# The first four units of chunk 0 in plain float32, block means from full value tiles, and a new order, in a fused attention and feed-forward kernel

## The chip, the cores and the metric

The kernel runs on one core of a Trainium2 chip. The metric is device time in microseconds (us), the median of several runs. The engines, as the profile names them: PE (TensorE; PEld is its loading of weights), DVE (VectorE), ACT (ScalarE), POOL (GpSimd) and SP (SyncE, which here issues nearly all transfers). Each works through its own list of instructions in order and waits on the others by semaphores.

## The reference, cut to what matters

Inputs: q, k, v of shape (4 batches, 8 heads, 768 tokens, 64), float32; w_in (512 x 2048) and w_out (2048 x 512), which arrive as float64.

```
k_sum = k in blocks of 32 tokens, max over the block        # 24 block keys per head
v_sum = v in blocks of 32 tokens, mean over the block       # 24 block values
scores = q.k / 8 where |i - j| < 16, else -1e9 ;  q.k_sum / 8 + log(32)
a = exp(scores - max) ; a = a / (sum(a) + 1e-9)
x = a @ concat(v, v_sum)                                    # 3072 tokens x 512 (8 heads x 64)
h = x @ w_in ;  g = h / (1 + exp(-h)) ;  out = g @ w_out
```

## The kernel before, in words

**Tiling.** A *stage* s is 128 tokens of all heads: batch b = s // 6, tile t = s % 6, 24 stages. A *chunk* c is two stages, 256 tokens; there are 12. A *unit* (c, f) is one chunk through one pair of 128-wide blocks of the hidden layer, f = 0 to 7. The units of chunks 0 to 3 come first, in the order chunk 0 f 0 to 3, chunk 1 f 0 to 3, chunk 1 f 4 to 7, chunk 0 f 4 to 7, then chunks 2 and 3; from chunk 4 on the chunks go in pairs with seven products in place of eight (another function). Stages 0 to 3 are called plain (`s < NPL`): their attention is in float32.

**Attention of a plain stage.** PE multiplies q by the local keys and by the block maxima `km` (scores, L722); the maxima come from DVE (L473) over K tiles that hold a whole batch of two heads. DVE adds the mask and takes the row maximum (L747), ACT takes the exponential (L751), PE transposes, ACT or DVE copies, and PE multiplies by the value tile (L792), whose last 24 rows are the block means. The sums of the exponentials are turned into factors, spread over the partitions by PE (`over`), copied to `xr`, and multiplied by the value product (L846): that is x.

**Block means.** `job_mean` (L630) adds six tiles of values times a small matrix of 1/32 into one bank on PE (L649) and takes each tile's largest absolute value on DVE (L652). For tiles 0 to 3 it reads the value tiles that attention uses too (`main_v`, L616), which hold 94 rows in two overlapping halves, so there are two matmuls to a tile, with the matrices `blocks0`, `blocks1` and `blocks2`; tiles 4 and 5 are loaded apart, 128 rows, one matmul each with `blocks`. The result is copied to `vms` (L653) and SP stores it into the value tiles (`side_v`, L625/626). The largest value gives the scale of x (`v_scale`).

**Weights.** A weight comes as float64, 1 MB. ACT rescales its top words (L922), one of three engines its low words (L923), DVE joins them to float32 (L924, `plain_w`). For the first layer the largest value follows (L940, PE L944, DVE L948), and from it a power of two `ur`; then the weight is split in two float16 halves (`split_w`, L956 and L957).

**A unit.** The first layer adds three float16 products (high x high, high x low, low x high; L1006, 24 matmuls of 256 columns to a unit). So x has two halves as well: `xh` (L848) and the remainder `xl` (L849), both in the scale taken from the means' values. ACT takes tanh(h/2) with its scale (L1020), DVE forms (1 + tanh) * h (L1021). In chunks 0 and 1, f below 4, ACT multiplies by `ur` (L1023) and the second layer is plain float32 with `plain_w` (L1015, 128x512); elsewhere g is split as x is and the second layer is three float16 products.

**What sets the order.** `Plan` collects operations, each with a cost for every engine that may run it. The string ORDER, three characters an operation, names the next operation and its engine; since it covers all 2679 operations it is replayed as it stands (`replay`). The costs then decide only how the lists of different engines are laid beside one another as they are issued, and how many filler matmuls (into bank 0, without use of their result) go between PE's operations until the first chunk has begun. SP's queue is in order as well. Buffers for loading (`staging`) are taken from weight buffers whose weights come later: `staging(-1)` and `staging(0)` name which.

SP's list before, from the start: q, K tiles, the value tiles between them, q, three more value tiles, the first weights (f 0 first layer and second layer, f 1 both); then the stores of `vms` into the value tiles, and the rest of the weights.

Of the kernel before, what the change touches and what calls it, by code (L numbers as in the profile page):

```python
# [21 lines left out]
P = 128  # L22
# [43 lines left out]
class Plan:  # L66
# [14 lines left out]
    DMA0 = 800.0  # L81
# [46 lines left out]
    def sweep(self, prio, on, back):  # L128
# [7 lines left out]
        free = {} if back else {"dma": self.DMA0}  # L136
# [122 lines left out]
def local_attn_ffn(ctx: ExitStack, tc: tile.TileContext, q0, qkT, qF, qkD, kF, v0, v, vR, w, out):  # L259
# [57 lines left out]
    blocks1 = const.tile([P, 11 * 4], F32, name="blocks1")  # L317
    blocks2 = const.tile([P, 11 * 4], F32, name="blocks2")
    nc.vector.memset(blocks1, 0.0)
    nc.vector.memset(blocks1[:, 19:24], 1.0 / BLK)  # L320
    edge = blocks1[:, 19:24]
    nc.gpsimd.affine_select(out=edge, in_=edge, pattern=[[-BLK, 5]], compare_op=ALU.is_ge, fill=0.0, base=BLK - HALO, channel_multiplier=1)
    nc.gpsimd.affine_select(out=edge, in_=edge, pattern=[[BLK, 5]], compare_op=ALU.is_ge, fill=0.0, base=HALO - 1, channel_multiplier=-1)
    nc.vector.memset(blocks2, 0.0)
    edge = blocks2[:, 22:24]
    nc.vector.memset(edge, 1.0 / BLK)
    nc.gpsimd.affine_select(out=edge, in_=edge, pattern=[[-17, 2]], compare_op=ALU.is_ge, fill=0.0, base=-2 * HALO, channel_multiplier=1)
    nc.gpsimd.affine_select(out=edge, in_=edge, pattern=[[17, 2]], compare_op=ALU.is_ge, fill=0.0, base=2 * HALO + 16, channel_multiplier=-1)
# [7 lines left out]
    nc.vector.tensor_copy(out=band[:, 0], in_=band[:, 1])  # L336
# [42 lines left out]
    nc.vector.memset(am_t, 0.0)  # L379
# [14 lines left out]
    tt_t = ring(NTT, [P, 4 * P], F16, "tt")  # L394
    xh_t = ring(NSUP, [P, NCT, CH], F16, "xh")
# [62 lines left out]
    def job_k(b, prio):  # L458
        prio += nudge("k", b)
        km = km_t[b % 2]  # L460
        for hp in range(4):
            prio += 0 if b else nudge("kh", hp)
            stg, key = staging(None if b else -1)
            kf = stg[:, :S]
            if b == 0:
                plain_k[hp] = stg[:, :S + 2 * HALO], key
                kf = stg[:, HALO:HALO + S]
                for side in (stg[:, :HALO], stg[:, HALO + S:S + 2 * HALO]):
                    (nc.vector if hp < 2 else nc.gpsimd).memset(side, 0.0)
                if hp == 3:  # L470
                    nc.vector.memset(band[:HALF, 0, :HALO], NEG)
# [39 lines left out]
    def job_km(b, prio):  # L511
# [7 lines left out]
        plan.op({"dve": 240}, sums, r=[("qsc", b % 2)], w=[("mask", i) for i in range(3)], prio=prio)  # L519
# [64 lines left out]
    def job_qk(s, prio):  # L584
# [8 lines left out]
        if b == 0:  # L593
# [4 lines left out]
            plan.op({"pool": 400, "act": 270, "dve": 150}, lambda e: copy(e, qk[:, :, P + HWIN:P + NKEY], km_t[0]), r=[("km", 0, hp) for hp in range(4)], w=keys, prio=prio)  # L598
# [8 lines left out]
        plan.op({"pool": 400, "act": 270, "dve": 150}, lambda e: copy(e, kr[:, :, HWIN:NKEY], km_t[b % 2]), r=[("km", b % 2, hp) for hp in range(4)], w=key, prio=prio)  # L607
# [13 lines left out]
    def side_v(t, prio):  # L621
# [6 lines left out]
        plan.op({"dma": 480}, sums, r=["vms"], w=key[1:], prio=prio, cols=1520)  # L628

    def job_mean(prio):  # L630
        prio += nudge("mean")
        k = sbank()
        for t in range(NTILE):
            at = (NTILE - 1 - t) * 4
            if t < NPL:
                main_v(t, prio)
                (vr, key), cost = plain_v[t], 1093
                key = key[:1]
                parts = [(vr[:HWIN, 0, :], blocks0[:HWIN] if t == 0 else blocks1[:HWIN, at:at + NB]), (vr[:HWIN, 1, :], blocks2[:HWIN, at:at + NB])]
# [11 lines left out]
            plan.op({"pe": 910 * len(parts) + 100}, mean, r=key, w=[("bank", k)], prio=prio, cols=2048)  # L651
# [5 lines left out]
    def job_vs(s, prio):  # L657
# [22 lines left out]
        plan.op({"act": 1050, "pool": 1080}, lambda e: times(e, v1, vr, vsc[:NKEY, 0:1]), r=key + [("vsc", b % 2)], w=[("v1", j)], prio=prio)  # L680
# [17 lines left out]
    def scores(s, quad):  # L698
# [30 lines left out]
        return go, need, {"pe": 820 if b else 990 if not plain else 620 if s < 2 else 1040}  # L729

    def job_a(s, quad, prio):
# [21 lines left out]
        if plain:  # L753
# [9 lines left out]
            plan.op({"act": 500, "dve": 600}, lambda e: copy(e, tt[:NKEY], tp), r=[("bank", k)], w=[ttk], prio=prio, port=())  # L763
# [7 lines left out]
        for i in range(4):  # L771
            plan.op({"dve": 160, "act": 310, "pool": 385}, lambda e, i=i: times(e, e4[:, i], e4[:, i], su[:, i:i + 1]), r=sk, w=es[i:i + 1], prio=prio)
        plan.op({"act": 580, "pool": 660}, lambda e: copy(e, hi, e4), r=es, w=pk[1:], prio=prio)
        plan.op({"dve": 570, "pool": 1090}, lambda e: less(e, lo, e4, hi), r=es + pk[1:], w=pk[:1], prio=prio)
# [4 lines left out]
    def job_c(s, prio):  # L779
        prio += nudge("c", s)  # L780
        av = bank[7]
        if s < NPL:
# [11 lines left out]
            plan.op({"pe": 1050}, direct, r=[ttk for _, ttk in quads] + key, w=[("bank", 7)], prio=prio, cols=2048)  # L794
# [23 lines left out]
    def job_x(s, prio):  # L818
# [10 lines left out]
        if s < NPL:  # L829
# [18 lines left out]
            plan.op({"act": 560}, lambda e: nc.scalar.copy(out=xh, in_=xr3), r=[("xr", s % 2)], w=[("xh", z, half)], prio=prio)  # L848
            plan.op({"dve": 680, "pool": 1280}, lambda e: less(e, xl, xr3, xh), r=[("xr", s % 2), ("xh", z, half)], w=[("xl", z, half)], prio=prio)  # L849
            return  # L850
        by, need = 1.0 / PSC, []
        plan.op({"act": 575}, lambda e: times(e, xh, x3, by), r=[("bank", k)] + need, w=[("xh", z, half)], prio=prio)
        plan.op({"dve": 661}, lambda e: rest_of(xl, x3, by, xh), r=[("bank", k), ("xh", z, half)] + need, w=[("xl", z, half)], prio=prio, port=())

    def pair_x(s, prio):
# [7 lines left out]
        plan.op({"act": 575, "dve": 600}, lambda e: times(e, plain, x3, by), r=[("bank", k)], w=[("xw", j, q, half) for q in range(2)], prio=prio, port=())  # L863
        for q in ((0, 1) if j == 0 else (1,)):
# [3 lines left out]
            plan.op({"act": 365}, lambda e, hi=hi, src=src: times(e, hi, src, by), r=[("bank", k)], w=[("xs", z, n, half)], prio=prio)  # L868
            plan.op({"dve": 370}, lambda e, hi=hi, lo=lo, src=src: rest_of(lo, src, by, hi), r=[("bank", k), ("xs", z, n, half)], w=[("xs", z, n, half, "low")], prio=prio, port=())
# [6 lines left out]
        for (to, in0, in1, op, own, n), more in zip(steps, reads):  # L876
            key = [("xw",) + own + (h,) for h in range(2)]
            plan.op({"dve": 640, "pool": 1157}, lambda e, to=to, in0=in0, in1=in1, op=op: eng[e].tensor_tensor(out=to, in0=in0, in1=in1, op=op),
                    r=[("xw",) + m + (h,) for m in more for h in range(2)], w=key, prio=prio)
            hi, lo = (xs_t[z][n][:, i].rearrange("p c t -> p (c t)") for i in range(2))  # L880
            plan.op({"act": 560}, lambda e, hi=hi, to=to: nc.scalar.copy(out=hi, in_=to), r=key, w=[("xs", z, n, h) for h in range(2)], prio=prio)
            plan.op({"dve": 690, "pool": 1280}, lambda e, hi=hi, lo=lo, to=to: less(e, lo, to, hi), r=key + [("xs", z, n, h) for h in range(2)], w=[("xs", z, n, h, "low") for h in range(2)], prio=prio)

    def sum_w(f, prio):
# [5 lines left out]
        if f < NSUP:  # L890
            parts = [wt[f, 0][:, i].rearrange("p j c -> p (j c)") for i in range(2)]
            plan.op({"pool": 2180, "dve": 1135}, lambda e: eng[e].tensor_tensor(out=wf, in0=parts[0], in1=parts[1], op=ALU.add), r=[("wh", f, 0), ("wl", f, 0)], w=own, prio=prio)
        for out, in0, in1, op in ((b22, b22, b12, ALU.subtract), (b12, b12, b11, ALU.subtract), (b11, b22, b11, ALU.add), (b21, b21, b11, ALU.subtract)):
            plan.op({"dve": 370, "pool": 640}, lambda e, out=out, in0=in0, in1=in1, op=op: eng[e].tensor_tensor(out=out, in0=in0, in1=in1, op=op), w=own, prio=prio)  # L894
        r = 1.0 if f < NSUP else ur_t[:, f, 1:2]
        hi, lo = (t.rearrange("p k c -> p (k c)") for t in wsum[f])
        plan.op({"act": 1050}, lambda e: times(e, hi, wf, r), r=own + [("ur", f)], w=to + [("ws", f)], prio=prio)
        plan.op({"dve": 1250}, lambda e: rest_of(lo, wf, r, hi), r=own + [("ur", f), ("ws", f)], w=to + [("wsl", f)], prio=prio)

    def job_w(fp, kind, prio):  # L900
# [7 lines left out]
        if wide:  # L908
# [14 lines left out]
            plan.op({"act": 1040, "dve": 690, "pool": 1200}, last_bits, r=mine, w=[("wb", fp, kind)], prio=prio)  # L923
# [552 lines left out]
```

## Time and profile before

| | |
|---|---|
| three runs | 595.00 to 595.84 us, median 595.16 us |
| profiled execution | 592.56 us, of which the span of the trace is 590.8 us |
| PE busy | 573.4 us, 97% of the span, 5924 instructions |
| DVE busy | 463.5 us, 78%, 1226 |
| ACT busy | 413.4 us, 70%, 982 |
| POOL busy | 225.6 us, 38%, 289 |
| moved | 78.97 MB, mean 134 GB/s |

```profile
## 2 busy tenths in 40 slices
PE   7989899999999999989999999999999999999997
PEld 3377566666776667666766566676666666588886
DVE  5698988887887988977567686986586767789885
ACT  1498999887676788868576886876767765466640
POOL 2026441253145222124564442342621554275442
PEclk7699999999999999999999999999999999999999
DMA  8879982436454449435723468353365021100002
```

Each column is a fortieth of the span, some 14.8 us, and each digit a busy share in tenths (9 is 90% or more). PEclk is the clock that PE was granted, in tenths of full speed. PE is nearly full everywhere, with a lower clock in the first two slices; the other engines are busier in the first third than later, and the transfers are dense up to about 90 us.

### The profile page before, as it was taken

Reading aid. Unit: us, or ns where it says so; the run is one execution under the profiler, and the core shown is the slowest. Engines: PE = TensorE matmul, PEld = TensorE weight load, DVE = VectorE, ACT = ScalarE, POOL = GpSimd, SP = SyncE. Lnnn points to the kernel's source line nnn. Section 1 sums busy time; section 2 is a strip of 40 time slices with the busy share of each in tenths; the row PEclk is TensorE's granted clock in tenths of the full one; section 3 lists DMA queues with packets and bytes.
Section 4 is the critical chain, followed back from the end, with each engine's and each line's share of the span. In section 5 each row is a group of like instructions: output and inputs, shape, how many; then the busy total and the mean of one; then the engine's idle time right before and its main releaser. Section 6 shows DMA issues by size and latency. Waiting matters only on the chain. (4 is left out here: it accounts for less than half of the span.)

```text
span 590.8 us, 15367 instructions
## 1 busy us (share of the span) xinstructions
PE 573.4 (97%) x5924; PEld 397.7 (67%) x5924; DVE 463.5 (78%) x1226; ACT 413.4 (70%) x982; POOL 225.6 (38%) x289
## 2 busy tenths in 40 slices
PE   7989899999999999989999999999999999999997
PEld 3377566666776667666766566676666666588886
DVE  5698988887887988977567686986586767789885
ACT  1498999887676788868576886876767765466640
POOL 2026441253145222124564442342621554275442
PEclk7699999999999999999999999999999999999999
DMA  8879982436454449435723468353365021100002
GB/s 256 331 252 384 339 311 82 81 80 160 125 175 118 114 131 208 91 107 140 176 65 89 155 180 198 126 114 87 122 152 139 34 55 21 71 1 1 2 3 71
DMA packets 64921, 78.97 MB, mean 134 GB/s; under 512 B 46288, under 2 KB 48336, under 8 KB 62800
## 3 DMA queue, kind: packets, MB, share of 16 engines
q1 hardware_dynamic: 64704, 77.86, 46.2%
q8 instruction: 46, 0.75, 0.5%
q14 instruction: 27, 0.22, 0.1%
q10 hardware_dynamic: 144, 0.13, 0.1%
HBM read 58.83 MB, written 6.29 MB: 110 GB/s over the span
## 5 line engine op out<-in xcount | busy, mean ns | idle before, releaser
L1077 PE MATMUL bank<-wt 128*128 128x256 f16 x1248 | 152.3, 273 | 2.7 <-DVE t L1057 1.2
L1077 PEld LDWEIGHTS <-wt 128*128 128x128 f16 x1248 | 121.4, 98 | 32.8 <-issue 3.9
L1015 PE MATMUL bank<-wt,g 128*128 128x512 f16 (+1 forms) x352 | 97.7, 420 | 0.9 <-ACT g L273 0.8
L751 ACT ACTIVATE e<-e,mx 128x118 f32<-128x118 f32 x192 | 73.3, 383 | 35.8 <-DVE mx L747 35.4
L1006 PE MATMUL bank<-xh,wt 128*128 128x256 f16 x512 | 91.2, 273 | 0.0
L1006 PEld LDWEIGHTS <-wt 128*128 128x128 f16 x768 | 74.7, 98 | 18.4 <-issue 4.2
L1006 PE MATMUL bank<-xl,wt 128*128 128x256 f16 x256 | 69.8, 273 | 0.0
L1128 PE MATMUL bank<-wt,g 128*128 128x512 f16 x288 | 69.4, 379 | 0.3 <-DVE g L283 0.3
L1056 ACT ACTIVATE t<-bank,asc 128x512 f32<-128x512 f32 x48 | 32.3, 683 | 23.7 <-PE bank L1077 16.3
L747 DVE CUSTOM_DVE_ANT_0 e<-bank,masks,qsc 128x118 f32<-128x118 f32 x144 | 42.3, 336 | 6.9 <-PE bank L722 4.9
L1128 PE MATMUL bank<-wt,xl 128*128 128x512 f16 x192 | 46.0, 379 | 0.0
L1057 DVE SCALAR_TENSOR_TENSOR t<-t,bank 128x512 f32<-128x512 f32 x48 | 32.4, 684 | 17.3 <-ACT t L1056 17.3
L1015 PEld LDWEIGHTS <-g 128*128 128x128 f16 x288 | 27.7, 98 | 27.0 <-DVE g L283 0.3
L1128 PEld LDWEIGHTS <-g 128*128 128x128 f16 x288 | 27.7, 98 | 26.0 <-DVE g L283 0.7
L283 POOL TENSOR_TENSOR g<-t,g 128x512 f16<-128x512 f32 x22 | 26.4, 1199 | 37.9 <-ACT g L1058 11.5
L275 POOL TENSOR_SCALAR e<-e,sum 128x118 f32<-128x118 f32 x50 | 21.7, 444 | 45.4 <-DVE sum L766 33.7
L751 ACT ACTIVATION_READ_ACCUMULATOR e<-e,mx 128x1 f32 x192 | 36.1, 188 | 0.0
L1020 ACT ACTIVATE t<-bank,asc 128x512 f32<-128x512 f32 x32 | 21.8, 681 | 13.9 <-PE bank L1006 13.7
L1128 PEld LDWEIGHTS <-xl 128*128 128x128 f16 x192 | 18.7, 98 | 17.4
L1021 DVE SCALAR_TENSOR_TENSOR t<-t,bank 128x512 f32<-128x512 f32 x32 | 21.8, 683 | 10.6 <-ACT t L1020 10.5
L894 POOL TENSOR_TENSOR wt<-wt 128x256 f32<-128x256 f32 x20 | 16.1, 810 | 36.8 <-DVE wt L280 12.8
L283 POOL TENSOR_TENSOR p<-e,p 128x472 f16<-128x472 f32 x16 | 16.7, 1047 | 34.7 <-DVE vv L280 12.9
(272 smaller groups left out, 1206.3 us busy)
## 6 DMA issues: line engine op xcount, KB each, us to landing
wt<-in_w_dram SPq DMA_DIRECT2D x16, 1024.0 KB
raw<-in_qkD_dram SPq DMA_DIRECT2D x18, 620.0 KB
raw<-in_v_dram SPq DMA_DIRECT2D x20, 512.0 KB
out_dram<-raw SPq DMA_DIRECT2D x20, 256.0 KB
raw<-in_kF_dram SPq DMA_DIRECT2D x12, 384.0 KB
raw<-in_qF_dram SPq DMA_DIRECT2D x9, 512.0 KB
raw<-in_vR_dram SPq DMA_DIRECT2D x12, 384.0 KB
raw<-vms SPq DMA_DIRECT2D x40, 48.0 KB
```

Of the source, the lines that this page charges most:

```text
L275: nc.gpsimd.tensor_scalar(out=out, in0=in_, scalar1=by, scalar2=0.0, op0=ALU.mult, op1=ALU.add)
L283: eng[e].tensor_tensor(out=out, in0=in0, in1=in1, op=ALU.subtract)
L747: plan.op({"dve": 195 if b == 0 else 255}, lambda e, k=k, at=at, et=et, mx=mx: nc.vector.tensor_tensor_reduce(out=et, in0=bank[k][:, at:at ...
L751: plan.op({"act": 375}, lambda e, et=et, mx=mx, total=total: nc.scalar.activation(out=et, in_=et, func=AF.Exp, scale=-1.0, bias=mx, accum_ ...
L1006: nc.tensor.matmul(out=h[:, d * CH:(d + 1) * CH], lhsT=wt[f, 0][:, part, d, ct * P:(ct + 1) * P], rhs=x[:, ct, :], start=(ct == 0 and q == ...
L1015: nc.tensor.matmul(out=bank[to][:, :z0 - a0], lhsT=a[:, d * CH + u * P:d * CH + u * P + P], rhs=b[:, d, a0:z0], start=(opens and d == 0 an ...
L1020: plan.op({"act": 640}, lambda e: nc.scalar.activation(out=t, in_=h, func=AF.Tanh, scale=asc_t[c // 3 % 2][:, f:f + 1]), r=[("bank", k), ( ...
L1021: plan.op({"dve": 605}, lambda e: nc.vector.scalar_tensor_tensor(out=t, in0=t, scalar=1.0, in1=h, op0=ALU.add, op1=ALU.mult), r=[("bank", ...
L1056: plan.op({"act": 640}, lambda e: nc.scalar.activation(out=t, in_=h, func=AF.Tanh, scale=asc_t[c // 3 % 2][:, f:f + 1]), r=[("bank", k), ( ...
L1057: plan.op({"dve": 605}, lambda e: nc.vector.scalar_tensor_tensor(out=t, in0=t, scalar=1.0, in1=h, op0=ALU.add, op1=ALU.mult), r=[("bank", ...
L1077: nc.tensor.matmul(out=to, lhsT=w2[part][:, ct * P:(ct + 1) * P], rhs=xs[j][:, x, ct, :], start=(opens and ct == 0 and q == 0), stop=(ct = ...
L1128: nc.tensor.matmul(out=bank[to], lhsT=a[:, d * CH + v * P:d * CH + v * P + P], rhs=wt[f, 1][:, b][:, d, :], start=(opens and d == 0 and q ...
```

## The change

1. **Block means.** All six value tiles are loaded apart for the means, as 128 full rows, and multiplied by `blocks`: six matmuls. `blocks0`, `blocks1`, `blocks2` and the zeroing of `am` go. The loads of the tiles for attention (`main_v`) come later in the order, and `side_v` waits for the load of its tile as well.
2. **Bare units** (c = 0, f below 4). x is formed unscaled in float32 in a new tile `xp`; the first layer is 8 matmuls of 256 columns in float32 from `plain_w`; tanh has the constant scale 0.5, DVE writes g itself, and the multiplication by `ur` goes. The chunk's sum is scaled by 0.5 where it is put aside. `xh` and `xl` of chunk 0, for its units f 4 to 7, are made from `xp` after it, and the split weights for other chunks.
3. **Engines.** More operations may run on POOL (splits and copies); many cost numbers change; `SETUP` gives each engine a start time in the planner's account. In the new ORDER 350 operations have another engine than before; operations per engine go from 963 to 968 on DVE, 733 to 719 on ACT, 240 to 245 on POOL, and the transfers from 241 to 245.
4. **Buffers.** The K tiles are staged in other weight buffers (`staging(-7)`), the memsets beside them are all on DVE, and the copy of the mask's first half comes behind them.
5. **ORDER** is new throughout. SP's list now begins: value tile 1, K 2, K 3, q, value tile 0, K 0, value tile 2, K 1, q, value tile 3, three q, value tiles 4 and 5, the weight of f 0; then the value tiles for attention 0 and 1, the weight of f 1, the store of `vms` for stage 0, tile 2, the store for stage 1, two q, the second layer of f 0, the values of stage 4, the store for stage 2, the weight of f 2, the second layer of f 1, the weights of f 3. PE's list ahead of the first unit: scores of stage 0 (second half of the heads), three means, a transpose, scores of stage 0 (first half), a mean, scores of stage 1, a mean, transpose, mean, transpose, scores of stage 1, the weight's scale, `over` of stage 0, scores of stage 2, transpose, `over` of stage 1, transpose, the value product of stage 0, transpose, `over` of stage 2, the value product of stage 1, scores of stage 3, the weight's scale. The value product of stage 2 comes after the first unit's first half.

The core of the diff (the string of ORDER, the host's layout and edits that change only cost numbers are left out but for examples):

```diff
-    DMA0 = 800.0
+    SETUP = {"dma": 800.0, "dve": 3900.0, "act": 2500.0, "pool": 3600.0}
...
-            stg, key = staging(None if b else -1)
+            stg, key = staging(None if b else -7)
...
-        plan.op({"dma": 480}, sums, r=["vms"], w=key[1:], prio=prio, cols=1520)
+        plan.op({"dma": 480}, sums, r=["vms"] + key[:1], w=key[1:], prio=prio, cols=1520)
...
             if t < NPL:
-                main_v(t, prio)
-                (vr, key), cost = plain_v[t], 1093
-                key = key[:1]
-                parts = [(vr[:HWIN, 0, :], blocks0[:HWIN] if t == 0 else blocks1[:HWIN, at:at + NB]), (vr[:HWIN, 1, :], blocks2[:HWIN, at:at + NB])]
-                src = vr[:HWIN].rearrange("p a c -> p (a c)")
-            else:
-                stg, key = staging(-1)
-                src, cost = stg[:, :DM], 603
-                parts = [(src, blocks[:, at:at + NB])]
-                plan.op({"dma": 680}, lambda e, src=src, t=t: nc.sync.dma_start(out=src, in_=v0[t - NPL]), w=key, prio=prio)
+                main_v(t, prio + 5)
+            stg, key = staging(-1)
+            src, cost = stg[:, :DM], 603
+            parts = [(src, blocks[:, at:at + NB])]
+            plan.op({"dma": 680}, lambda e, src=src, t=t: nc.sync.dma_start(out=src, in_=v0[t]), w=key, prio=prio)
...
+            if c == 0:
+                half_x = xp[:, :, half * P:half * P + P]
+                plan.op({"act": 510, "dve": 600}, lambda e: copy(e, xr, bank[rb]), r=[("bank", rb)], w=[("xr", s % 2)], prio=prio, port=())
+                plan.op({"dve": 620}, lambda e: nc.vector.tensor_tensor(out=half_x, in0=x3, in1=xr.rearrange("p (c t) -> p c t", c=NCT), op=ALU.mult), r=[("bank", k), ("xr", s % 2)], w=[("xp", half)], prio=prio, port=())
+                plan.op({"act": 512, "pool": 705}, lambda e: times(e, xh, half_x, vsc_t[0][:, 0:1]), r=[("xp", half), ("vsc", 0)], w=[("xh", z, half)], prio=prio + 20)
+                plan.op({"dve": 625}, lambda e: rest_of(xl, half_x, vsc_t[0][:, 0:1], xh), r=[("xp", half), ("vsc", 0), ("xh", z, half)], w=[("xl", z, half)], prio=prio + 20)
+                return
...
-        plan.op({"act": 1050}, lambda e: times(e, hi, wf, by), r=[("wv", fp, kind)] + need, w=[("wp", fp, kind), ("wh", fp, kind)], prio=prio)
+        plan.op({"act": 1050, "pool": 1150}, lambda e: times(e, hi, wf, by), r=[("wv", fp, kind)] + need, w=[("wp", fp, kind), ("wh", fp, kind)], prio=prio)
...
+        bare = c == 0 and f < QF
...
+            def bare_go(e):
+                for ct in range(NCT):
+                    nc.tensor.matmul(out=h[:, d * CH:(d + 1) * CH], lhsT=plain_w[f, 0][:, d, ct * P:(ct + 1) * P], rhs=xp[:, ct, :], start=ct == 0, stop=ct == NCT - 1)
...
+        need_x = [("xp", half) for half in range(2)] + [("wv", f, 0)] if bare else [(x, z, half) for x in ("xh", "xl") for half in range(2)] + [("wh", f, 0), ("wl", f, 0)]
...
+        half_z = 0.5 if bare else asc_t[c // 3 % 2][:, f:f + 1]
+        to_t, tk = (g, [("gh", n), ("gl", n)]) if bare else (t, [("t", j)])
...
+        if bare:
+            pass
+        elif plain:
+            plan.op({"act": 600, "pool": 705}, lambda e: times(e, g, t, ur_t[:, f, 0:1]), r=[("t", j), ("ur", f)], w=[("gh", n), ("gl", n)], prio=at - TUNE["post"])
```

## Rows read from the trace of the kernel before

**Rows 1.** Busy time by stretches: start:end, length, each engine's busy us (instructions), PEclk, DMA share, GB/s

```profile
10.00:15.00 5.00, 5.00 (x38) 1.61 (x36) 2.52 (x11) 1.64 (x8) 0.00 (x0) 0.50 1.03 261
20.00:25.00 5.00, 5.00 (x13) 2.04 (x12) 2.42 (x7) 0.99 (x3) 0.00 (x0) 0.50 1.02 405
30.00:35.00 5.00, 5.00 (x108) 4.33 (x108) 4.16 (x11) 4.60 (x15) 0.00 (x0) 1.00 0.38 90
60.00:70.00 10.00, 8.30 (x67) 4.35 (x66) 9.15 (x13) 9.15 (x13) 4.45 (x8) 1.00 0.98 382
100.00:120.00 20.00, 20.00 (x115) 12.57 (x113) 17.45 (x42) 18.03 (x40) 5.85 (x10) 1.00 0.39 76
250.00:300.00 50.00, 47.83 (x550) 33.30 (x547) 34.44 (x99) 34.58 (x90) 22.52 (x24) 1.00 0.51 134
```

**Rows 2.** The same for PE alone, by 1 us: PE busy, PEclk, DMA share, GB/s

```profile
8.00:9.00 1.00, 0.10 (x4) 0.83 1.06 381
25.00:26.00 1.00, 1.00 (x2) 0.64 1.04 425
```

**Rows 3.** PE in order of time: start, duration, line, operation; in brackets a wait before

```profile
8.90 0.42 PE L722 MATMUL bank<-km,qk 64*64 64x24 f32 x8 [2.60 <-DVE km L473]
...
15.06 7.02 PE L649 MATMUL bank<-wt,blocks 94*24 94x512 f32 x8
...
29.04 1.04 PE L649 MATMUL bank<-wt,blocks 128*24 128x512 f32 x2
...
51.41 0.27 PE L1006 MATMUL bank<-xh,wt 128*128 128x256 f16 x1
...
58.63 1.98 PE L1015 MATMUL bank<-wt,g 128*128 128x512 f32 x4 [0.79 <-ACT g L273]
...
62.32 1.28 PE L792 MATMUL bank<-wt 118*64 118x64 f32 x32 [1.70 <-DMA wt<-vms]
...
86.42 1.04 PE L722 MATMUL bank<-qk 64*64 64x118 f32 x32 [0.57 <-DVE qk L269]
...
92.00 3.60 PE L1015 MATMUL bank<-wt,g 128*128 128x512 f32 x8
...
95.43 0.27 PE L1006 MATMUL bank<-xh,wt 128*128 128x256 f16 x1
...
96.74 1.88 PE L1015 MATMUL bank<-wt,g 128*128 128x512 f32 x4
```

**Rows 4.** SP's queue in order of time: when a transfer was issued, and how long that took

```profile
18.55 0.56 SPq L912 DMA_DIRECT2D wt<-in_w_dram  x1
...
30.71 1.68 SPq L626 DMA_DIRECT2D wt<-vms  x2
```

**Rows 5.** SP's waits from 0 to 120 us, the longest: us in total, times, longest

```profile
SPq L626 <- ACT e L751: 11.6, 1, 11.6
```

**Rows 6.** DVE, ACT and POOL in order of time, as for PE

```profile
6.50 0.35 DVE L366 COPY masks<-masks 128x118 f32<-128x118 f32 x2 [1.07 <-POOL masks L362]
...
10.75 0.94 DVE L473 TENSOR_REDUCE km<-wt 128x24 f32<-128x768 f32 x1
...
12.32 0.39 ACT L751 ACTIVATE e<-e,mx 128x118 f32<-128x118 f32 x1
...
18.39 1.11 ACT L922 ACTIVATE wt<-wt 128x1024 f32<-128x1024 f32 x1
...
27.53 0.28 DVE L747 CUSTOM_DVE_ANT_0 e<-bank,band 128x118 f32<-128x118 f32 x1 [5.00 <-PE bank L722]
...
30.11 0.57 ACT L265 COPY vms<-bank 24x512 f32<-24x512 f32 x1
...
44.29 0.68 DVE L846 TENSOR_TENSOR xr<-bank,xr 128x512 f32<-128x512 f32 x1
...
47.58 0.60 ACT L848 CAST xh<-xr 128x512 f16<-128x512 f32 x1
...
49.62 1.16 POOL L283 TENSOR_TENSOR xl<-xr,xh 128x512 f16<-128x512 f32 x1 [2.74 <-ACT wt L932]
```

More of the change, by code (lines that the diff above doesn't have):

```diff
@@ L135, in sweep @@
         end, chosen = [0.0] * n, [None] * n
-        free = {} if back else {"dma": self.DMA0}
+        free = {} if back else dict(self.SETUP)
         shared = 0.0
@@ L517, in sums @@
                 nc.vector.tensor_scalar(out=m, in0=lg[:HALF].unsqueeze(2).to_broadcast([HALF, 3, NB]), scalar1=qs[:HALF, 3:4], scalar2=None, op0=ALU.add)
-        plan.op({"dve": 240}, sums, r=[("qsc", b % 2)], w=[("mask", i) for i in range(3)], prio=prio)
+        plan.op({"dve": 460}, sums, r=[("qsc", b % 2)], w=[("mask", i) for i in range(3)], prio=prio)
     def am_sum(n, prio):
@@ L728, in scores @@
             need.append(("qkk", s % 2))
-        return go, need, {"pe": 820 if b else 990 if not plain else 620 if s < 2 else 1040}
+        return go, need, {"pe": 760 if b else 990 if not plain else 640 if s < 2 else 1100}
     def job_a(s, quad, prio):
@@ L862, in pair_x @@
         plain = xw[j].rearrange("p (c t) -> p c t", c=NCT)[:, :, at]
-        plan.op({"act": 575, "dve": 600}, lambda e: times(e, plain, x3, by), r=[("bank", k)], w=[("xw", j, q, half) for q in range(2)], prio=prio, port=())
+        plan.op({"act": 495, "dve": 600}, lambda e: times(e, plain, x3, by), r=[("bank", k)], w=[("xw", j, q, half) for q in range(2)], prio=prio, port=())
         for q in ((0, 1) if j == 0 else (1,)):
@@ L1016, in ffn2 @@
             return go
+        turn = [("turn", i - APART)] if i >= APART else []
+        need_x = [("xp", half) for half in range(2)] + [("wv", f, 0)] if bare else [(x, z, half) for x in ("xh", "xl") for half in range(2)] + [("wh", f, 0), ("wl", f, 0)]
         for d in range(2):
-            plan.op({"pe": 1310}, ffn1(d), r=[(x, z, half) for x in ("xh", "xl") for half in range(2)] + [("wh", f, 0), ("wl", f, 0)] + ([("turn", i - APART)] if i >= APART else []), w=[("bank", k)], prio=at + nudge("f1", i), cols=3072)
@@ L1020, in job_f @@
-        plan.op({"act": 640}, lambda e: nc.scalar.activation(out=t, in_=h, func=AF.Tanh, scale=asc_t[c // 3 % 2][:, f:f + 1]), r=[("bank", k), ("asc", c // 3 % 2, f)], w=[("t", j)], prio=at - TUNE["post"])
-        plan.op({"dve": 605}, lambda e: nc.vector.scalar_tensor_tensor(out=t, in0=t, scalar=1.0, in1=h, op0=ALU.add, op1=ALU.mult), r=[("bank", k)], w=[("t", j)], prio=at - TUNE["post"], port=())
-        if plain:
-            plan.op({"act": 600}, lambda e: times(e, g, t, ur_t[:, f, 0:1]), r=[("t", j), ("ur", f)], w=[("gh", n), ("gl", n)], prio=at - TUNE["post"])
-        else:
-            plan.op({"act": 540}, lambda e: nc.scalar.copy(out=gh, in_=t), r=[("t", j)], w=[("gh", n)], prio=at - TUNE["post"])
-            plan.op({"pool": 1280, "dve": 690}, lambda e: less(e, gl, t, gh), r=[("t", j), ("gh", n)], w=[("gl", n)], prio=at - TUNE["post"])
+            plan.op({"pe": 1720 if bare else 1310}, ffn1(d), r=need_x + turn, w=[("bank", k)], prio=at + nudge("f1", i), cols=4096 if bare else 3072)
@@ new lines, in job_f @@
+        half_z = 0.5 if bare else asc_t[c // 3 % 2][:, f:f + 1]
+        plan.op({"act": 586}, lambda e: nc.scalar.activation(out=t, in_=h, func=AF.Tanh, scale=half_z), r=[("bank", k)] + ([] if bare else [("asc", c // 3 % 2, f)]), w=[("t", j)], prio=at - TUNE["post"])
+        to_t, tk = (g, [("gh", n), ("gl", n)]) if bare else (t, [("t", j)])
+        plan.op({"dve": 605}, lambda e: nc.vector.scalar_tensor_tensor(out=to_t, in0=t, scalar=1.0, in1=h, op0=ALU.add, op1=ALU.mult), r=[("bank", k)] + ([("t", j)] if bare else []), w=tk, prio=at - TUNE["post"], port=())
@@ L1220, in go @@
             for to, m, more, keep, reads in ((u2, 6, c11, k2, q11), (u3, 7, u2, k3, k2), (c12, 5, u2, q12, k2), (c22, 5, u3, q22, k3), (c11, 2, c11, q11, None), (c12, 3, c12, q12, None), (c21, 4, u3, q21, k3)):
-                plan.op({"dve": 350}, lambda e, to=to, m=m, more=more: nc.vector.scalar_tensor_tensor(out=to, in0=place(m), scalar=osc, in1=more, op0=ALU.mult, op1=ALU.add),
+                plan.op({"dve": 392}, lambda e, to=to, m=m, more=more: nc.vector.scalar_tensor_tensor(out=to, in0=place(m), scalar=osc, in1=more, op0=ALU.mult, op1=ALU.add),
                         r=[("bank", terms[m][2])] + ok + ([reads] if reads else []), w=[keep], prio=at2, port=())
```

242 lines of the change are left out of this document (114 added, 128 removed).

## The prediction

> **What bounds the kernel now.** I read the busy time by stretches first. From 100 us on PE is full (20.00 of 20.00 between 100 and 120) and where it is not, little is missing (47.83 of 50 between 250 and 300) [rows 1]. So behind the opening a microsecond is gained only by giving PE less to do, or by starting its stream sooner. The same view shows what the opening costs. [...] Between 30 and 35 the DMA share is 0.38 after 1.02 between 20 and 25 [rows 1]: the loads stop in the middle of the weights.
>
> PE's list in order of time, read next, gives the start of the feed-forward stream: the first L1006, chunk 0's first unit (U0 from here), is at 51.41 us [rows 3]. Behind it PE waits 0.79, 1.70 and 0.57 us and then hardly at all [rows 3]. So the path to 51.41 is what sets the end.
>
> That path begins with the block means. Their 94-row matmuls run at the low clock: four of them (eight records, two to a matmul) take 7.02 us from 15.06, 1.75 each; at full clock the last one takes 1.04 with its way through the array [rows 3]. The mean is copied to `vms` only at 30.11 [rows 6]. SyncE's queue is in order: behind the weight load at 18.55 stands the store of `vms` into the value tiles, which goes out at 30.71 [rows 4]; the waits give 11.6 us for it [rows 5], and that is the hole in the loads. After that x of stage 1 is multiplied at 44.29, cast at 47.58, and its remainder is taken on POOL at 49.62 to about 50.8 [rows 6]; U0 follows at 51.41.
>
> **The change part by part.**
>
> *Cost constants.* SETUP and the other numbers of the planner do nothing on the chip by themselves, since ORDER is given in full. They move only filler matmuls and the order of issue between engines. I take zero; what can come of fillers is the clock, below.
>
> *PE's work.* A bare unit has 8 fp32 matmuls of 256 columns in place of 24 fp16 ones. The trace has no fp32 matmul of 256 columns in this line. [...] I take 0.43: 3.43 us for 2.62, four times, +3.2 us (+3.5 at 0.44). Ten mean matmuls become six, but they lie ahead of U0 and count in its start. In the new list of PE stage 2's value product comes behind U0's first matmuls instead of ahead of them: the one at 62.32 takes 1.28 with its drain, +1.2 us [rows 3].
>
> *The start of U0.* It needs the plain x of stages 0 and 1 and the decoded weight, no longer the scale of x, the two fp16 halves of x, or the weight's scale and halves. Behind the multiply of stage 1, which ends at 44.97, that takes away the way to 50.78, 5.8 us, at once [rows 6].
>
> The rest comes from the means. DVE gets to the K maxima earlier: the mask edges, which waited 1.07 us at 6.50, move back [rows 6], and some small setup goes. I put the first pair of maxima (0.87 each in a row of them) at 5.4 to 7.1 us, and PE's first whole scores at 7.2 in place of 8.90 [rows 3, 6]. The six value tiles and four K tiles with the first queries are 3.7 MB; at 405 GB/s, with 2.5 us to the first, they are there by 12 us, at 261 by 17 [rows 1]. The new list has three means, the transposes of stage 0, the other half of its scores, and three more means between other work. Their order is set by the eight exponentials of stage 0 and four of stage 1 on ACT (0.39 each) and copies of 0.57 [rows 6], with DVE's reductions between: the last mean ends at about 16 and `vms` is copied at about 17.5, 12.6 us earlier. So SyncE's 11.6 us wait is all but gone.
>
> From there to U0: on ACT one weight pass (1.11), twelve exponentials (4.7) and four copies or scalings of half a tile (2.3) give 17.5 + 8.1 = 25.6 [rows 6]; then the value product of stage 1 (1.2) [rows 3] and the multiply (0.7) [rows 6], beside which stage 3's scores run: U0 at 28 if nothing waits. Engines hand over to each other some twenty times on this path, and in the trace before DVE alone waits 5.00 us for PE at 27.53 [rows 6]. I add 3.4 us, two thirds of that one wait, and take **31.4 us, 20.0 earlier**. Bounds: 28, and 45 if only the 5.8 us came.
>
> *More loads.* Four full tiles of 256 KB are added, about 1 MB or 2.6 us at 405 GB/s [rows 1]. They go ahead of the first weight, so that weight lands at about 14.5 us, still before ACT's list comes to it. In exchange the stall of 11.6 us ends, and the K tiles move out of the buffers of units 2 and 3, so those weights need not wait for stage 3's scores. From 25 us the loads lead by some 4 us. Cost nothing; if the hole returned, units 2 and 3 would be late by it.
>
> *Idle behind U0.* Here the cover is thin. ACT's list from stage 1's scaling to the tanh of the fourth unit has 18 full passes over a weight or value tile (1.11, some 1.06 with the overlap), 8 exponentials at 0.39, 4 tanh and 3 copies at about 0.6 [rows 6]: about 26 us, so that tanh ends at about 52. The fourth unit's first product ends on PE 18.8 us behind U0's start, at 50.2, and its second is asked for some 7 us later, so ACT is just in time. DVE has about 18 us of work between the first and the fourth unit's second step, in 15.3 us of PE's. Against 3.1 us of idle now [rows 3] I take 5, +1.9; from 1 (less than now) to 12.
>
> *More engines to choose from.* 350 operations change engine; the totals per engine hardly move (DVE 963 to 968 operations, POOL 240 to 245). From 250 us on I take zero, within 2 us either way.
>
> The sum: -20.0 + 3.2 + 1.2 + 1.9 = -13.7 us. The profiled execution took 592.56 us (span 590.8), so 578.9; the median of the three runs is 595.16, 2.6 above it, so **581.5 us**. With U0 between 28 and 35 this is 577 to 586.
>
> **The rivals.**
>
> *The clock stays low in the opening.* Before, it fell between 8 and 9 us (0.83), after PE had waited 2.60 us for the K maxima, and came back only between 25 and 26 (0.64) [rows 2, 3]. For it here: the means are still 24 columns wide, and a steady row of them from 15.06 to 22.08 did not raise it [rows 3]. Against: the wait shrinks, and fillers may cover it. PE's new list has about 16 us of work ahead of U0 at full clock (six means 5.1, the scores of four stages 4.7, transposes 3, two value products 2.4, the rest 1). At half rate from 8 to 25.7 us, 8.8 of it would be done; U0 comes at 33 plus the 3.4, about 36.5, and the time is 586.5.
> [...]
>
> *The lead is handed back.* ACT and DVE lists are nearly as long as PE's up to the twelfth unit. If they run at 85% in place of 95%, idle behind U0 is 12 us and U0 comes at 33: -18.4 + 3.2 + 1.2 + 8.9 = -5.1, 590. For it: they waited for each other, POOL and the loads all through the opening. Against: with the split of four weights gone from the path, PE has 7 us of other work there.
>
> *Slower: plain fp32 drops the clock.* Units 0 to 3 would now be 27.4 us of fp32 products in both layers. [...] For it: the fp32 means went with the low clock. Against: from 58.63 to 70 us PE did almost only fp32 products of 128x128 weights, with a gap of 1.70 us [rows 3], and the granted clock between 60 and 70 is 1.00 [rows 1].
>
> *It doesn't do what it says.* If U0 still waited for something late (its weight, or stage 1's values behind the queue) and began at 45, -6.4 + 3.2 + 1.2 + 1.9 leaves 595.
>
> **How the numbers follow.** Chances: forecast 0.55, low clock 0.24, handed back 0.12, slower 0.06, no start gained 0.03. The range 575 to 591 holds most of the first three: about 0.81. About 0.2%, 1.2 us, can be told from no change. Faster by more: 0.55 + 0.24 + 0.10 + 0.01 = 0.90; same 0.03 (split of the last and the third); slower 0.07.
>
> **What would show it.** Right: the first L1003 of the bare kind at 29 to 35 us; `vms` copied at 16 to 20; SyncE's longest wait for it under 3 us; no stretch of 5 us under 0.38 of DMA share before 60; a bare unit at 3.43 us of PE; under 8 us of PE idle between U0 and 100 us; PE at 1.00 through units 0 to 3. Wrong: a granted clock of 0.50 up to 25 us (the first rival), ACT or DVE at the end of PE's waits with 10 us or more (the second), U0 behind 40 us.

## The result, and the profile after

The changed kernel takes 576.54 us (median of 4, 573.90 to 577.57) against 595.23 for the kernel before (4 runs, 595.00 to 595.84); the ratio is 0.9678, interval 0.9643 to 0.9712. The profiled execution took 573.90 us (span 572.1) against 592.56: 18.7 us less by either measure, where 13.7 were forecast. In one experiment, a_old_mean, two of four executions (583 us) were disturbed and are left out of the ratio.

Busy time by stretches, and one stretch for PE alone (columns as in [rows 1, 2]):

```profile
10.00:15.00 5.00, 5.00 (x76) 2.22 (x76) 4.64 (x23) 3.19 (x15) 0.00 (x0) 1.00 1.08 401
20.00:25.00 5.00, 3.15 (x49) 2.23 (x42) 4.16 (x27) 5.00 (x24) 0.00 (x0) 1.00 0.89 273
30.00:35.00 5.00, 5.00 (x25) 4.43 (x26) 3.52 (x18) 3.68 (x8) 0.00 (x0) 1.00 1.02 370
100.00:120.00 20.00, 20.00 (x228) 14.23 (x227) 17.71 (x53) 18.49 (x50) 7.87 (x10) 1.00 0.41 111
```

```profile
30.00:80.00 50.00, 48.22 (x314) 1.00 0.95 359
```

The clock is 1.00 where it was 0.50 [rows 1], and between 30 and 35 us the loads run (DMA share 1.02 for 0.38). From 100 us on nothing has changed that matters.

PE in order of time:

```profile
8.07 2.85 PE L628 MATMUL bank<-wt,blocks 128*24 128x512 f32 x6
...
25.30 1.27 PE L771 MATMUL bank<-wt 118*64 118x64 f32 x32 [2.06 <-DMA wt<-vms]
...
30.10 5.43 PE L992 MATMUL bank<-xp,wt 128*128 128x256 f32 x24
35.46 1.15 PE L771 MATMUL bank<-wt 118*64 118x64 f32 x32
37.12 1.98 PE L1009 MATMUL bank<-wt,g 128*128 128x512 f32 x4 [0.51 <-DVE g L1019]
...
51.86 1.22 PE L771 MATMUL bank<-wt 118*64 118x64 f32 x32 [0.51 <-DMA wt<-vms]
...
69.81 1.98 PE L1009 MATMUL bank<-wt,g 128*128 128x512 f32 x4 [0.49 <-POOL g L275]
...
72.06 1.04 PE L701 MATMUL bank<-qk 64*64 64x118 f32 x32 [0.27 <-DVE wt L277]
```

U0 starts at 30.10 in place of 51.41, 21.3 us earlier. Twelve bare matmuls (24 records) take 30.10 to 35.46, 0.447 each, so 3.57 to a unit where three products took 2.62: +3.8 over four units. Stage 2's value product stands behind them: +1.15. PE then waits 0.51, 0.51, 0.49 and 0.27, 1.8 us against 3.1 [rows 3]: -1.3. That makes -17.65. The remaining 1.0 us is in PE's totals from U0 to the end: it is busy for 531.9 us against 527.5, so 4.4 more and not 4.95, and behind 100 us it is idle for 8.2 in place of 8.8.

ACT's copy of the means, and SP's queue with its longest wait:

```profile
16.69 0.57 ACT L265 COPY vms<-bank 24x512 f32<-24x512 f32 x1
```

```profile
12.64 0.90 SPq L603 DMA_DIRECT2D wt<-in_v_dram  x2
13.58 0.43 SPq L898 DMA_DIRECT2D wt<-in_w_dram  x1
20.29 1.68 SPq L610 DMA_DIRECT2D wt<-vms  x2
```

```profile
SPq L610 <- DMA wt<-in_v_dram: 17.1, 2, 10.9
```

The copy comes at 16.69 in place of 30.11 [rows 6]. But the store waits again, now for another thing: the value tile that it completes is loaded at 12.64, behind the first weight, and must have landed before its last rows are written. The queue stands from 14.0 to 20.3; up to 17.3, when the copy ends, the means would have held it too.

### The profile page after: what moved, and what is told of

Same layout as the page of the kernel before. It is cut to its first block, busy times and chain, and to the rows that moved or that the text cites. A ratio compares the mean times of both kernels' runs of the same rounds, so it can differ in the third digit from the quotient of the medians.

```text
span 572.1 us, 15129 instructions
## 1 busy us (share of the span) xinstructions
PE 557.5 (97%) x5809; PEld 390.7 (68%) x5809; DVE 457.4 (80%) x1242; ACT 407.2 (71%) x983; POOL 207.4 (36%) x258
## 4 chain that ended last, share of the span: by engine, by line
PE 45%; DMA 3%; ACT 2%; DVE 1%; issue 1%; SPq 1%; POOL 0%; DVEq 0%; ACTq 0%
PE bank L1077 19%; PE bank L1128 16%; PE bank L1199 6%; DMA tt<-p 2%; PE bank L789 2%; PE bank L701 1%; DMA out_dram<-raw 1%; DMA raw<-in_qkD_dram 1%; DMA raw<-vms 0%; ACT vv L273 0%; DVE t L1057 0%; ACT e L730 0%; SPq L649 0%; SPq L756 0%; DVE vv L280 0%
## 5 line engine op out<-in xcount | busy, mean ns | idle before, releaser
L1077 PEld LDWEIGHTS <-wt 128*128 128x128 f16 x1248 | 121.2, 98 | 33.9 <-issue 5.9
L1000 PE MATMUL bank<-xh,wt 128*128 128x256 f16 x448 | 80.6, 273 | 0.0
L1000 PEld LDWEIGHTS <-wt 128*128 128x128 f16 x672 | 65.0, 98 | 15.2 <-issue 2.6
L1000 PE MATMUL bank<-xl,wt 128*128 128x256 f16 x224 | 61.0, 273 | 0.0
L1056 ACT ACTIVATE t<-bank,asc 128x512 f32<-128x512 f32 x48 | 32.4, 681 | 26.5 <-PE bank L1077 19.4
L1128 PEld LDWEIGHTS <-g 128*128 128x128 f16 x288 | 27.8, 98 | 25.2
L1057 DVE SCALAR_TENSOR_TENSOR t<-t,bank 128x512 f32<-128x512 f32 x48 | 32.7, 684 | 14.8 <-ACT t L1056 14.5
L283 POOL TENSOR_TENSOR g<-t,g 128x512 f16<-128x512 f32 x26 | 30.0, 1158 | 24.8 <-ACT g L265 8.5
L275 POOL TENSOR_SCALAR e<-e,sum 128x118 f32<-128x118 f32 x49 | 20.0, 417 | 49.7 <-DVE sum L745 37.1
L265 ACT CAST g<-t 128x512 f16<-128x512 f32 x43 | 26.2, 611 | 7.0 <-DVE t L1019 5.2
L1128 PEld LDWEIGHTS <-xl 128*128 128x128 f16 x192 | 18.7, 98 | 17.6
L283 DVE TENSOR_TENSOR g<-t,g 128x512 f16<-128x512 f32 x28 | 20.1, 717 | 7.2 <-ACT g L265 4.1
L1103 DVE TENSOR_TENSOR bank<-bank,xh 128x256 f32<-128x256 f32 x32 | 13.7, 429 | 15.0 <-PE bank L1077 14.4
```

The costliest lines, as they stand in the source:

```text
L265: nc.scalar.copy(out=out, in_=in_)
L275: nc.gpsimd.tensor_scalar(out=out, in0=in_, scalar1=by, scalar2=0.0, op0=ALU.mult, op1=ALU.add)
L283: eng[e].tensor_tensor(out=out, in0=in0, in1=in1, op=ALU.subtract)
L1000: nc.tensor.matmul(out=h[:, d * CH:(d + 1) * CH], lhsT=wt[f, 0][:, part, d, ct * P:(ct + 1) * P], rhs=x[:, ct, :], start=(ct == 0 and q == ...
L1056: plan.op({"act": 586}, lambda e: nc.scalar.activation(out=t, in_=h, func=AF.Tanh, scale=asc_t[c // 3 % 2][:, f:f + 1]), r=[("bank", k), ( ...
L1057: plan.op({"dve": 605}, lambda e: nc.vector.scalar_tensor_tensor(out=t, in0=t, scalar=1.0, in1=h, op0=ALU.add, op1=ALU.mult), r=[("bank", ...
```

## The experiments

**Is it the clock?** b_fill is the kernel before with more fillers ahead of the first scores:

```diff
+        first = True
...
+            if fills and first:
+                fills, first = fills + (14), False
```

> The kernel before with 14 more filler matmuls ahead of the first scores, so that PE does not stand idle there. My theory (the full clock is one part of the gain among several): the granted clock stays at 1.00 from 8 to 25 us, the 94-row means take 0.9 us each in place of 1.75, and the time is 588 to 591 us, 4 to 7 less than before's 595.2; the rest of the gain stays away. Rival (the gain is the clock): 580 or less. Rival (the clock falls whatever stands ahead of the scores): 595, clock 0.50 from 10 to 25.

588.62 us, ratio 0.9869 (0.983 to 0.9908). Stretch and PE rows of b_fill:

```profile
10.00:15.00 5.00, 4.35 (x41) 1.39 (x40) 3.44 (x16) 2.02 (x10) 0.00 (x0) 1.00 1.05 261
```

```profile
12.99 3.61 PE L652 MATMUL bank<-wt,blocks 94*24 94x512 f32 x8 [0.65 <-DMA wt<-in_v_dram]
...
46.51 0.27 PE L1009 MATMUL bank<-xh,wt 128*128 128x256 f16 x1
```

The same eight records take 3.61 us in place of 7.02 [rows 3] and U0 comes at 46.51, 4.9 earlier. Fourteen fillers buy 1.3%: the clock is worth that much in the kernel before, as the theory had it, and not the whole gain.

a_gap goes the other way, the changed kernel with `fills + (-13)` in the same place:

> The changed kernel with 13 of its first 24 filler matmuls left out, so that PE stands idle for some 3 us ahead of the first scores, as it did before. My theory: the granted clock falls to 0.50 at about 9 us and comes back near 25; chunk 0's first unit starts at 35 in place of 30.1 and the time is 581 to 582 in place of 576.5. Rival (the clock does not follow that wait, or the opening has the slack for it): 576 to 577.

577.67 us, 0.9685 (0.9641 to 0.9728): no loss. PE, and one of its microseconds:

```profile
7.15 0.59 PE L704 MATMUL bank<-wt,qk 64*64 64x94 f32 x8 [3.26 <-DMA qk<-in_q_dram]
...
8.35 4.75 PE L631 MATMUL bank<-wt,blocks 128*24 128x512 f32 x6
...
29.71 5.43 PE L995 MATMUL bank<-xp,wt 128*128 128x256 f32 x24
```

```profile
9.00:10.00 1.00, 1.00 (x2) 1.00 1.04 383
```

After a wait of 3.26 us the means run slowly (4.75 us for six records, 2.85 without the wait, so 1.9 us lost), but by 13 us PE is at its pace again (eight records of scores take 0.60 us from 7.67 and 0.39 from 13.61), and U0 is not late: the 2.06 us that it waited for the store (above) swallow the loss. My theory was wrong here on both counts, how long the slow stretch lasts and that the opening has no slack.

**Which part of the change?** Four kernels make a square. a_old_mean and a_old_units undo one part in the lists of the changed kernel, what is needed earlier being brought forward; p_old_units and p_neither have lists worked out anew for the first 900 operations. In all four x of chunk 0 is formed in `xp`. The runs lie on three chips; each ratio is taken against the kernel before on the same chip, so differences between runs are best read from the ratios. The edits, besides ORDER: the first of these stands in a_old_mean and p_neither, the second in a_old_units, p_old_units and p_neither.

```diff
-            stg, key = staging(-1)
-            src, cost = stg[:, :DM], 603
-            parts = [(src, blocks[:, at:at + NB])]
...
+                (vr, key), cost = plain_v[t], 1093
...
+                parts = [(vr[:HWIN, 0, :], blocks0[:HWIN] if t == 0 else blocks1[:HWIN, at:at + NB]), (vr[:HWIN, 1, :], blocks2[:HWIN, at:at + NB])]
...
-        bare = c == 0 and f < QF
+        bare = False
```

> The changed kernel with the means taken as before, from the 94-row value tiles with two matmuls each (ten in all); the rest of the order stands. Theory: four more matmuls at the full clock (3.4 us) and longer maxima on DVE (2 us) bring the copy of the means to about 20 us in place of 16.7, but the store no longer waits for a second load of the tile (issued at 20.3 now); the first unit starts 1 to 3 us later, 577.5 to 580. Rival (the means are the main part of the gain): 584 or more. Rival (the means cost nothing beside the loads): 576.5 or less.

> The same kernel as a_old_mean, whose four executions lay at 573 and at 583: whether it is faster than the changed kernel (573 to 574, as its profile) or slower (583), or equal within 0.5% as the theory has it that the means by themselves no longer set the end: 575 to 579.

> The changed kernel with chunk 0's first four units in three float16 products again, each waiting for the halves of x and of its weight, and with the multiplication by ur; every operation that they need is brought forward on its engine. Theory: the first unit starts 3 to 5 us later and the next ones wait for splits on ACT and DVE, while PE saves 3.8 us: 579 to 584. Rival (the plain units carry nearly all of the gain): 588 or more. Rival (their path is hidden and only PE's work counts): 573.

> The changed kernel with chunk 0's first four units in three float16 products again, as in a_old_units, but with the order and the engines of the first 900 operations worked out anew for it (a search that moves operations within their dependencies, by the planner's own costs). My theory now: a_old_units lost its 19 us because its lists were made for the plain units (PE waited for the splits of the second unit while the loads stood still), not because three products cost that much; with lists of its own the first unit starts 3 us later and PE saves 3.8 us of work: 576 to 582. Rival (the plain units carry nearly all of the gain, whatever the order): 588 or more.

> The changed kernel with both parts undone (means from the 94-row tiles, three-product units), and with the order and engines of the first 900 operations worked out anew in the same way: what is left of the change is the order, the fillers and the buffers. Theory (the new order, with the clock that it keeps, is the larger part): 578 to 584, granted clock 1.00 up to 100 us. Rival (means and plain units are the gain): 590 or more.

> The changed kernel itself once more, as the measure for the others on this chip: 575 to 578 us, first unit at 30 us.

| | means from 94-row tiles | means from full tiles |
|---|---|---|
| three products | p_neither 581.26 us, 0.9744 (0.9704 to 0.9785), U0 at 39.60 | p_old_units 582.70, 0.9770 (0.9728 to 0.9812), U0 at 32.27 |
| plain float32 | a_old_mean_again 573.41, 0.9625 (0.9593 to 0.9657), U0 at 31.69; a_old_mean 0.9621 (0.9573 to 0.9670) | a_same 576.99, 0.9668 (0.9628 to 0.9707), U0 at 31.20 |

The first unit's rows, in p_neither, p_old_units and a_old_mean_again:

```profile
39.60 0.28 PE L1022 MATMUL bank<-xh,wt 128*128 128x256 f16 x1
```

```profile
32.27 0.27 PE L1000 MATMUL bank<-xh,wt 128*128 128x256 f16 x1
```

```profile
31.69 2.62 PE L1014 MATMUL bank<-xp,wt 128*128 128x256 f32 x11
```

Three things follow. With neither part, 2.6 of the 3.2% are there: most of the gain is the new order with its engines, fillers and buffers. With the plain units the kernels are faster by 1.0 to 1.2%, in either column; but the lists of the upper row come from another search than those of the lower, so how much of that is the units and how much the lists is not shown. The new means bring nothing: both rows are slower by 0.3 to 0.5% with them, though the intervals overlap, so a cost is not clear of noise. Against what was expected, a_old_mean came out faster than its range and p_old_units just above its own; and p_neither's clock was not 1.00 all the way:

```profile
10.00:15.00 5.00, 5.00 (x54) 2.79 (x56) 2.53 (x4) 0.59 (x1) 0.00 (x0) 0.50 1.05 286
```

The start of U0 is a poor measure between these lists, since they put different work behind it. A later mark is the first matmul of the chunk pairs: from there to the end the trace has 3439 PE instructions in each of these kernels. It stands at 229.11 us in a_old_mean_again, and in the changed kernel, a_same, p_old_units and p_neither at:

```profile
228.82 0.82 PE L1077 MATMUL bank<-wt 128*128 128x256 f16 x6
```

```profile
233.69 0.82 PE L1077 MATMUL bank<-wt 128*128 128x256 f16 x6
```

```profile
231.51 0.82 PE L1077 MATMUL bank<-wt 128*128 128x256 f16 x6
```

```profile
231.78 0.82 PE L1099 MATMUL bank<-wt 128*128 128x256 f16 x6
```

p_neither starts U0 7.3 us behind p_old_units and is only 0.3 behind it here: p_old_units has 3.2 us more of PE's work and 3.8 more of idle time in between. The two profiles of the changed kernel are 4.9 apart, with p_neither between them. Behind the mark p_neither takes 3.4 and p_old_units 7.5 us longer than the changed kernel; why is not shown.

a_old_units, in lists that were not made for it, took 595.47 us, 1.0000 (0.9966 to 1.0035), outside its expected range. The stretch from 60 to 70 us of its profiled execution, the slowest of its ten:

```profile
60.00:70.00 10.00, 5.94 (x43) 4.30 (x43) 5.35 (x7) 5.41 (x8) 1.34 (x2) 0.83 0.03 11
```

No engine is busy for more than 6 of the 10 us and the loads stand at a share of 0.03: the lists wait, for one another as it seems. The same work in lists of its own (p_old_units) takes 12.8 us less. What this run lost says little about the price of three products; the rival that the plain units carry it all falls.

b_new_mean puts the new means alone into the kernel before; the edit is the diff's own for `job_mean`, with the value tiles for attention loaded behind.

> The kernel before with the new means alone (six full tiles; the value tiles for attention are loaded behind them), all else in its order. Theory: four matmuls fewer on PE at the low clock, 1.75 us each, are 7 us on the way to the copy of the means; it comes at 24 to 27 in place of 30.1 and the time is 589 to 592. Rival (the loads or the maxima set that way, or the later value tiles take it back): 594 to 596.

591.21 us, 0.9911 (0.9878 to 0.9944), which is what was expected, but not by the way expected. ACT, SP's third store and PE:

```profile
21.83 0.56 ACT L265 COPY vms<-bank 24x512 f32<-24x512 f32 x1
```

```profile
35.05 1.50 SPq L609 DMA_DIRECT2D wt<-vms  x2
```

```profile
51.26 0.27 PE L984 MATMUL bank<-xh,wt 128*128 128x256 f16 x1
```

The copy is 8.3 us earlier than in [rows 6] (the clock is 1.00 from 5 to 25 us here too), the third store only 1.8, and U0 stands where it stood. The profiled execution, 594.16, is the slowest of its eight, so where the others gained 4 us is not shown.

**Do the new means cost something?** The profiled execution of a_same took 579.0 us. PE, a stretch of it, and ACT's longest waits from 21 to 100 us:

```profile
40.48 3.42 PE L1009 MATMUL bank<-wt,g 128*128 128x512 f32 x4 [2.77 <-DVE g L1019]
```

```profile
40.00:42.00 2.00, 1.52 (x2) 0.50 0.98 410
```

```profile
ACT wt L908 <- DMA wt<-in_w_dram: 5.1, 3, 3.5
ACT wt L902 <- DMA wt<-in_w_dram: 3.7, 1, 3.7
```

The first store went out at 22.44 there, 2.2 us later than in the first profile; the weights queued behind it came late, ACT waited 8.8 us for four of them, PE waited 2.77 for a unit's g, and the clock fell behind that wait. In a_old_mean_again the tile has landed when the means are ready:

```profile
21.14 3.20 SPq L627 DMA_DIRECT2D wt<-vms  x4
```

and up to 100 us ACT waits for no weight (0.6 us for a tile of queries is all that it waits for loads), and PE, from U0 on, for nothing. U0 is 0.5 us later than in a_same and the median 3.6 us earlier. But a_same's profiled execution is the slowest of its six (573.0 to 579.0). In the first profile of the same kernel ACT waited 4.9 us for five weights and PE 0.51 us at this place, and that execution took 573.90, as good as a_old_mean_again's 573.60. So the chain is what one of the changed kernel's longer executions shows; why it comes in one and not in another, and whether it is the whole of the difference, was not tried: a_v94, which was to try it, did something else.

**Does U0's start set the end?** a_late has fillers ahead of it:

```diff
+            for _ in range(40 if i == 334 else 0):
+                self.fill()
```

> The changed kernel with 40 filler matmuls (some 4.4 us of PE) right ahead of chunk 0's first unit, so that this unit starts at 34.5 to 35.5 in place of 30 to 31. If the start of this unit sets the end, as the prediction had it, the time grows by 4.4 us to 581.4; if what follows is bound by the weights' way through ACT and DVE (a_old_mean started 2 us later and ended no later), the idle time behind it goes and the time grows by 2.6 or less: 577 to 579.6.

580.79 us, 0.9766 (0.9724 to 0.9808): 3.8 us more than a_same by the medians, 5.8 by the ratios. U0 and the mark of the chunk pairs:

```profile
34.30 1.89 PE L994 MATMUL bank<-xp,wt 128*128 128x256 f32 x8
```

```profile
230.16 0.82 PE L1079 MATMUL bank<-wt 128*128 128x256 f16 x6
```

U0 is 3.1 later than in a_same, 4.2 later than in the first profile. By the times a later start costs about what it was expected to. The trace says less: at the mark 1.3 of the 4.2 us are left, PE is idle nowhere in between (1.8 us in the first profile), and the rest of the loss of this execution, 3.6 us, lies behind the mark, where p_neither and p_old_units lost theirs too. So the start of U0 counts, but that it counts in full is not shown, and the rival of the slack is not settled. The prediction's frame, in which the start of U0 sets the end, holds for the step from 51 us to 30; between 30 and 40 the square shows that it does not.

**The engines.** a_no_pool changes ORDER alone, six passes from POOL to ACT.

> The changed kernel with six passes over the first weights (three splits, three passes over low words) back from POOL on ACT, in their place of the order. If more engines to choose from is worth something in the opening (ACT's list is just in time for the fourth unit), 6.6 us more on ACT give 2 to 6 us of idle time on PE: 579 to 583. If ACT has the slack: 577.

579.26 us, 0.9718 (0.9680 to 0.9755). PE:

```profile
39.48 1.99 PE L1009 MATMUL bank<-wt,g 128*128 128x512 f32 x4 [2.27 <-DVE g L1019]
```

2.3 us above a_same by the medians, 3.0 by the ratios, with overlapping intervals. A wait of that size was in the profile of a_same too, so the price is 0 to 3 us and not settled.

**The store without its wait.** a_v94:

```diff
-        plan.op({"dma": 1000}, lambda e: nc.sync.dma_start(out=plain_v[t][0][:VROW], in_=v[0, t, :VROW]), w=key, prio=prio)
+        plan.op({"dma": 1000}, lambda e: nc.sync.dma_start(out=plain_v[t][0][:HWIN], in_=v[0, t, :HWIN]), w=key[:1], prio=prio)
...
-        plan.op({"dma": 480}, sums, r=["vms"] + key[:1], w=key[1:], prio=prio, cols=1520)
+        plan.op({"dma": 480}, sums, r=["vms"], w=key[1:], prio=prio, cols=1520)
```

> The changed kernel with value tiles of 94 rows for attention, so that the stores of the means write other rows than the load and no longer wait for it on SP's queue (6.3 us for the first store). Theory: the first store goes out at 17.5 in place of 20.3, PE's wait of 2.06 us for it goes, the first unit starts 1 to 2 us earlier; since the start counts only in part, the time is 575 to 577 against 577.0. Rival (the store was on the path that sets the end): 574.5 or less.

603.26 us, 1.0133 (1.0103 to 1.0163). PE, a stretch, and SP:

```profile
35.73 1.98 PE L771 MATMUL bank<-wt 118*64 118x64 f32 x32 [13.64 <-DMA wt<-vms]
```

```profile
25.00:30.00 5.00, 0.00 (x0) 0.00 (x0) 0.00 (x0) 0.00 (x0) 0.00 (x0) 0.50 0.18 63
```

```profile
16.62 4.36 SPq L610 DMA_DIRECT2D wt<-vms  x2
21.02 0.42 SPq L603 DMA_DIRECT2D wt<-in_v_dram  x1
21.50 7.73 SPq L610 DMA_DIRECT2D wt<-vms  x2
```

The store goes out at 16.62, but with tiles of 94 rows (376 KB) on the queue the loads come at a crawl: for five microseconds no engine does anything and the loads run at a share of 0.18 and 63 GB/s, where the changed kernel, with its 96-row tiles among other loads, ran at 1.04 and 383 GB/s from 12 to 16 us. Why they come so slowly is not shown. So the run tests a slow load, and what the store's wait costs stays open.

## Why the prediction was right, and where its reasons were not

- *The start of U0*: forecast 31.4, between 28 and 45; measured 30.10 and 31.20. Right. That it sets the end held for these 21 us (18.7 at the end, the rest accounted for above), and not between lists that start U0 at 30 to 40.
- *What brings it there*: forecast 5.8 us for the splits and "the rest comes from the means". Here the step fails. With neither part U0 comes at 39.60, 11.8 us earlier than before; either part alone brings it to about 32, both to 30 or 31. The two are not terms to be added: both shorten the same stretch, and what then stands in the way is, as I read it, the store. The 11.8 are the clock, the lists and the buffers. My estimate of the clock's share is 4.9 at most, what b_fill gained, since p_neither still shows 0.50 from 10 to 15 us; the rest was not taken apart further.
- *SyncE's wait "all but gone", under 3 us*: wrong. I saw the wait go with its cause and did not ask what the same instruction waits for next, though the change itself adds the landing of its tile to what `side_v` reads. It stood for 6.3 us, 3.0 of them behind the copy, and 10.9 for a later store.
- *More loads, "cost nothing"*: the bytes fit, the place in the queue did not. By the square the kernels with the new means are slower by 0.3 to 0.5%, within the noise, though their copy comes earlier: it brought nothing.
- *PE's work*: 3.57 us to a bare unit for 3.43, so +3.8 for the forecast +3.2, and 1.15 for 1.2. Right in kind, 0.6 too small. The 0.43 of the forecast is half of a float32 matmul of 512 columns, four of which take 3.43 us from 92.00 to 95.43 [rows 3]; what the 0.44 beside it rests on no run shows, and a bare matmul took 0.447.
- *Idle behind U0*: forecast 5, with bounds 1 to 12; measured 1.8 in the profiled execution and 2.8 in a_same up to 100 us, so the rival of the lead handed back (12) falls. This term is 3.2 of the 5 us by which the sum fell short. ACT was even later than I had it (the fourth tanh at 56.59, not 52), but PE's list asks for what follows it only at 65.50, where I had it at about 57. PE does the second steps of the second and third unit in between, from 53.00 on. The rows of ACT and PE:

```profile
56.59 0.57 ACT L1017 ACTIVATE t<-bank 128x512 f32<-128x512 f32 x1
```

```profile
65.50 1.88 PE L1009 MATMUL bank<-wt,g 128*128 128x512 f32 x4
```

- *Plain float32 drops the clock*: no. 1.00 through 30 to 80 us in the first profile; in a_same it fell behind a wait of 2.77 us, to 0.50 from 40 to 42 us and 0.65 from 42 to 44, and was 1.00 from 44 to 52.
- *The clock stays low in the opening*: it did not stay low. The price forecast, 5 us, is near the 4.9 by which b_fill moved U0 in the kernel before. In the changed kernel a_gap's short slow stretch cost 1.9 us of PE's time ahead of U0 and nothing at the end; what a slow stretch up to 25 us would have cost it no run shows. In a_gap PE was back at its pace by 13 us, 6 us after its wait ended at 7.15.
- *More engines*: zero was taken; 0 to 3 us by a_no_pool.

So the total came out within the range because the start of U0 was read from resources (ACT's list, the loads) and not from the two edits to which I then put it down. That it came so near is in part luck: more than half of the earlier start comes without either edit, and that was in no term of the sum.

## What to carry to other kernels

Undo each part of a change in lists made for what is left; undone in lists made for the whole, a part looks as dear as the whole gain (595 for 583 here). When a wait goes because its cause comes earlier, look for the next thing that the same instruction needs, and for what is queued behind it. And run the version that the square points to: the plain units with the old means, 573.4 us, came out fastest of all, 3.7% below the kernel before, though its interval overlaps that of the changed kernel.

## What the runs showed of the hardware

A granted clock of 1.00 in the profile does not show that PE runs at its pace: in a_gap it reads 1.00 from 5 to 15 us while six records of matmuls after the wait took 4.75 us in place of 2.85. The run that left two rows of 96 out of its loads (94 rows) and the wait out of its stores, a_v94, took 603.26 us against 576.99 in a_same, 26 us longer, more than the whole change brought. And there PE waited three times for the stores of the means, 25.2 us in all and 13.64 at the longest, where it waited 2.06 and 0.51 us for them in the changed kernel.
